# A pre-norm attention and gMLP block on one core: gated values kept in the gate's rows, other memory for the late operands, and program order on four engines to the end

## The chip, the cores and the metric

The kernel runs on 1 core of one Trainium2 chip. The metric is the device time of one execution in microseconds. The core's engines are PE (matrix products, with PEld for its weight loads), DVE, ACT and POOL (elementwise work), and SP, which here only issues transfers.

## The reference

One sequence of 2048 tokens of width 640 passes two blocks in fp32. The change touches the second block alone:

```python
def _A_ref(x, wqkv, wo): ...      # 32 heads of 20, causal window of 256, softmax, projection
def _B_ref(x, w_in, w_sp, b_sp, w_out):
    z = _gelu(jnp.einsum("bsd,df->bsf", x, w_in))           # 640 -> 1728
    z1 = z[..., :Fh]                                        # Fh = 864
    z2 = _layernorm(z[..., Fh:], axis=-1)
    g = jnp.einsum("ts,bsf->btf", w_sp, z2) + b_sp[None, :, None]   # 2048 x 2048 over tokens
    return jnp.einsum("bsf,fd->bsd", z1 * g, w_out)         # 864 -> 640
h = x + _A_ref(_layernorm(x), wqkv, wo)
h2 = h + _B_ref(_layernorm(h), w_in, w_sp, b_sp, w_out)
```

## The kernel before

Tokens lie in 16 tiles of 128. Every fp32 operand is split into a high part (`hi`, a copy on ACT) and a remainder (`lo`, a subtraction on DVE), and every product is three matmuls (high by high, high by low, low by high) into one PSUM bank. The big products use seven block products in place of eight; their operands are named B11, T1, T2, B22, T3, B21, T4.

The attention and the projection run first. Then the second block runs as a list `steps`: each step has a function that writes PE's matmuls and one, the post, that empties their bank. `at(n, f)` hangs other work (loads, copies, subtractions) on a step's number; `run(n)` writes first what hangs on n, then the matmuls of step n, then its post. The steps are:

- 0 to 63: `z_pair`, eight tile pairs, 8 steps each: the first halves z1 of z, written to `z1_d` in memory.
- 64 to 79: `z2_pair`, four pairs (0 to 3), 4 steps each. A step is 15 matmuls of 432 columns into one of four banks of tag "a". Its post is a gelu on ACT into a row buffer (`row`). The statistics of a row (`stat`, on DVE and POOL), its normalisation on ACT (`norm`) and the copies, remainders and subtractions for the seven pieces (`right_blocks`, into `zc`) hang on the steps behind. The operands of the next tile (`prep`: a copy into `aw` from `fx`, and the remainder) hang on steps before.
- 80 to 135: `first_gate`, eight pairs of row tiles of w_sp, 7 steps of 12 matmuls: the gate's products over the first half of the tokens, written to `g_d`. The copies, sums and remainders of w_sp (`preps`) go into `aw`, raw tiles into `fx`. They hang on steps up to 9 before the pair.
- 136 to 151: `z2_pair` again, pairs 12 to 15, over the second half of the tokens.
- 152 to 207: `second_gate`: the products over the second half, added on DVE to the rows read back from `g_d`; then `gated` adds the bias and multiplies with z1, which is loaded into the two buffers `z1` (printed as z); the result is stored to `y_d`. The preparation of w_out hangs on 31 of these steps.
- 208 to 263: `out_pair`, eight pairs, 7 steps: y is turned by transposes on PE, split, multiplied with w_out, and added to h.

Which order the engines get is set in two ways. Inside `manual_schedule`, PE, DVE, ACT and SP take the instructions in the order in which the code writes them. Behind `ms.close()` a list scheduler reorders them by its own estimates. Before the change that happens at step 62, so that all from the first z2 pair on is in the scheduler's order. An engine takes its instructions in the final order, one by one, each when its semaphores allow.

The block below prints the functions that the change touches and their callers.

Of the kernel before, what the change touches and what calls it, by code (L numbers as in the profile page):

```python
# [15 lines left out]
P = 128  # L16
# [18 lines left out]
def block_kernel(ctx, tc, x, xt, wqk, wv, wo, w_in, wsp, bsp, w_out, out):  # L35
# [89 lines left out]
    def view(flat, lo, *shape):  # L125
        n = 1
        for d in shape:
            n *= d
        names = "abcd"[:len(shape)]
        return flat[:, lo:lo + n].rearrange(f"p ({' '.join(names)}) -> p {' '.join(names)}",  # L130
                                            **dict(zip(names, shape)))
# [675 lines left out]
    def minus(out, a, b, eng=None):  # L807
        plus(out, a, b, OP.subtract, eng)

    def copy(out, a):  # L810
        nc.scalar.activation(out, a, AF.Copy)  # L811
# [86 lines left out]
    def open_d():  # L898
        early_stack.close()
        base_stack.close()  # L900
        zp = pool(zc_stack, "zc")
        z = [zp.tile([P, 2, HF], F32R, name=f"ze{n}") for n in range(12)] + zl
        zc.extend([z[7 * k:7 * k + 7] for k in range(4)])
        wp = pool(win_stack, "win2")
        win2.append(wp.tile([P, 2, KD, FH], F32R, name="win2"))

    def open_e1():
        win_stack.close()
# [111 lines left out]
    def z2_pair(q, i, j, k):  # L1020

        n0 = len(steps)
        f0 = 2048 if q == 12 else 0
        r = [view(fx, f0 + (2 * k + t) % 3 * D, D) for t in range(2)]
        a = [view(aw, 3328 + (2 * k + t) % 3 * 2 * D, 2, KD, P) for t in range(2)]
        z = [row(), row()]

        def prep(t, first):
            r3 = r[t].rearrange("p (k t) -> p k t", k=KD)
            if first:  # L1030
                copy(a[t][:, 0], r3)
            else:
                minus(a[t][:, 1], r3, a[t][:, 0].bitcast(F32))

        def prod(t, h, b):
            b.append(bank("a", f"zb{q}_{t}_{h}"))
            for kk in range(KD):
                for x, y in ((0, 0), (0, 1), (1, 0)):
                    nc.tensor.matmul(b[0][:, :HF], a[t][:, x, kk], win2[0][:, y, kk, h * HF:(h + 1) * HF],  # L1039
                                     start=kk + x + y == 0, stop=kk == KD - 1 and x == 1)  # L1040

        def gelu(t, h, b):
            with tc.high_priority() if q == 15 else ExitStack():
                nc.scalar.activation(z[t][:, h * HF:(h + 1) * HF], b.pop()[:, :HF], AF.Gelu_apprx_tanh)

        for t, tile_t in ((0, i), (1, j)):
            m = n0 + 2 * t
            soon = k == 0 and q > 8
            at(m - (8 if soon else 12 if k == 0 else 6), lambda t=t, tile_t=tile_t: nc.sync.dma_start(r[t], hn_d[tile_t]))
            at(m - (2 - t if soon else 3), lambda t=t: prep(t, True))  # L1050
            at(m - (1 if soon else 2), lambda t=t: prep(t, False))
        for t in range(2):
            for h in range(2):
                steps.append((lambda t=t, h=h, b=(b := []): prod(t, h, b), lambda t=t, h=h, b=b: gelu(t, h, b)))
        blocks = [x[:, h * HF:(h + 1) * HF] for x in z for h in range(2)]
        stats = [None, None]

        def stat(t, h):
            if h == 0:
                stats[t] = stat_tiles(f"z{q}_{t}")  # L1060
            st, mv = stats[t]
            nc.vector.bn_stats(out=st[:, h, :], in_=blocks[2 * t + h])
            if h:
                stats_of(mv, st)

        def norm(t):
            scaled(z[t], z[t], stats[t][1])

        f = right_blocks(lambda: zc[k], *blocks)
        def soon(n, *fs):  # L1070
            def run_all():
                with tc.high_priority() if q == 15 else ExitStack():
                    for x in fs:
                        x()

            at(n, run_all)

        soon(n0 + 1, lambda: stat(0, 0))
        soon(n0 + 2, lambda: stat(0, 1))
        soon(n0 + 3, lambda: stat(1, 0), lambda: norm(0), *f[:3])  # L1080
        soon(n0 + 4, lambda: stat(1, 1), lambda: norm(1), f[3])
        soon(n0 + 5, *f[4:])
# [4 lines left out]
    def gate_pair(p, c, post, extra):  # L1087

        n0 = len(steps)
        if p == 0:  # L1090
            e_start.append(n0)
        f0 = (p + 1) % 2 * 2048
        a11, a12, a21, a22 = (view(fx, f0 + o, 4, P) for o in (0, 512, 1024, 1536))
        s1 = view(tmp1, 0, 4, P)
# [19 lines left out]
        def s4():  # L1114
# [5 lines left out]
                 (-3, lambda: (s2(), lo(T1, s1), hi(T2, a11))), (-2, lambda: (lo(T2, a11), hi(T3, a21))),  # L1120
                 (-1, lambda: (lo(T3, a21), hi(B21, a12))), (0, lambda: (s4(), hi(T4, a22))),
                 (1, lambda: (lo(B22, a12), lo(T4, a22)))]
        if p == 0:
            preps = [(-9, lambda: hi(B11, a11)), (-8, lambda: (lo(B11, a11), s13())), (-7, lambda: (s2(), hi(T1, s1))),
                     (-6, lambda: (lo(T1, s1), hi(T2, a11))), (-5, lambda: lo(T2, a11)), (-4, lambda: hi(B21, a12)),
                     (-3, lambda: lo(B21, a12)), (-2, lambda: minus(a12, a12, a11)),
                     (0, lambda: (hi(B22, a12), hi(T3, a21))), (1, lambda: lo(B22, a12)),
                     (2, lambda: (lo(T3, a21), hi(T4, a22))), (3, lambda: lo(T4, a22))]
        if p == 1:
# [1 line left out]
                     (-2, lambda: (s2(), lo(T1, s1), hi(T2, a11))), (-1, lambda: (lo(T2, a11), hi(T3, a21))),  # L1131
                     (0, lambda: (lo(T3, a21), hi(B21, a12), s4(), hi(T4, a22))),
                     (1, lambda: (lo(B22, a12), lo(T4, a22)))]
        at(n0 - 11 if p != 1 else n0 - 10, load)
        for m, f in preps:
            at(n0 + m, f)

        def prod(m, half, start, stop):
            if m in (B11, T1):
# [215 lines left out]
    def second_gate(p):  # L1355
# [10 lines left out]
        def gated(n):  # L1366
            t, c = (p + 8, j) if n > 20 else (p, i)
            z = e1["z1"][c % 2][:, HF * (n % 10 - 1):HF * (n % 10)]
            nc.vector.scalar_tensor_tensor(out=z, in0=g[n], scalar=bcol[:, t:t + 1], in1=z, op0=OP.add, op1=OP.mult)

        def load_z(n):
            nc.sync.dma_start(e1["z1"][n % 2], z1_d[tile_of(n)])

        at(n0 - (5 if p else 1), lambda: nc.sync.dma_start(gi, g_d[p]))
        for c in (1, 0):
            at(n0 - (4 if p else 0), lambda c=slice(c * HF, (c + 1) * HF): nc.sync.dma_start(gj[:, c], g_d[p + 8][:, c]))
        at(n0 + (1 if p else 0), lambda: load_z(i))
        at(n0 + (2 if p else 0), lambda: load_z(j))
        at(n0 + (4 if p else 5), lambda: gated(12))
        at(n0 + (5 if p > 1 else 6), lambda: gated(22))  # L1380
        at(n0 + 6, lambda: gated(11))
        at(n0 + 7, lambda: gated(21))
        for t in range(2):
            at(n0 + 6 + t, lambda t=t: nc.sync.dma_start(y_d[p + 8 * t], e1["z1"][t]))
        gate_pair(p, 1, [add(11), add(22), add(12), add(12), add(22), add(11), add(21)], lambda m: None)
        if p == 0:
            for k in range(4):
# [91 lines left out]
    for n in range(len(steps)):  # L1479
        run(n)  # L1480
        if n == 0:
            turn_h(NT - 2)
        if n == 1:
            scale_h(NT - 1)
        if n == 5:
            turn_h(NT - 1)
        if n == 62:
            ms.close()
        if n == 6:
            open_d()  # L1490
            w2p = win2_prep(view(fx, 4 * D + 256, FH))
        if n > 10:
            next(w2p, None)
# [30 lines left out]
```

## Time and profile before

| | |
|---|---|
| median of 3 runs | 1121.25 us (1114.17 to 1122.6) |
| profiled execution | 1122.61 us, span 1120.9 us |
| mean granted clock of PE | 0.998 |
| busy PE / PEld / DVE / ACT / POOL | 1079.9 / 972.4 / 801.1 / 585.1 / 317.3 us |

Busy shares are of the span. A row with two numbers at its start gives start and duration in us; "x3" means three instructions merged; what stands in brackets is how long the engine was idle before, and which engine, tile and line released it. Matmuls are pipelined: one of 432 columns lasts 0.36 us in a row, but the next starts 0.2 us behind it.

### The profile page before, as it was taken

What the parts mean: (1) busy time and instruction counts of PE and PEld (TensorE: products, weight loads), DVE (VectorE), ACT (ScalarE), POOL (GpSimd) and SP (SyncE); (2) the same over time, 40 slices, a digit from 0 to 9 for tenths busy, and PEclk for the clock granted to TensorE, in tenths of its full rate; (3) what the DMA queues carried; (4) which work ended last, traced back from release to release, by engine and by line L of the source; (5) the groups of instructions that cost most, each with busy time, mean ns of one, the idle gap of its engine ahead of it and who ended that gap; (6) DMA issues with size and microseconds to landing.
All of it is one profiled execution on the core that took longest, in us unless ns stands there. A gap on an engine that the chain in (4) does not pass through costs nothing.

```text
span 1120.9 us, 28796 instructions
## 1 busy us (share of the span) xinstructions
PE 1079.9 (96%) x11083; PEld 972.4 (87%) x11083; DVE 801.1 (71%) x2185; ACT 585.1 (52%) x1202; POOL 317.3 (28%) x447
## 2 busy tenths in 40 slices
PE   8999999999998999998999999999999899999998
PEld 8998887667887787798899999999999798898998
DVE  6643444789998998697777678655458988787684
ACT  4444443259998899644566567433347532233231
POOL 4324446776676677632200011000001000000000
PEclk9999999999999999999999999999999999999999
DMA  7833667545665555789545422233241477656542
GB/s 244 297 113 119 173 185 266 172 162 180 185 191 179 179 172 168 189 256 315 208 167 196 157 88 76 86 123 111 99 156 57 161 217 262 205 189 238 176 139 94
DMA packets 92282, 194.74 MB, mean 174 GB/s; under 512 B 11952, under 2 KB 46272, under 8 KB 88256
## 3 DMA queue, kind: packets, MB, share of 16 engines
q1 hardware_dynamic: 92144, 192.90, 53.3%
q8 instruction: 87, 1.43, 0.5%
q14 instruction: 51, 0.42, 0.1%
HBM read 127.90 MB, written 64.95 MB: 172 GB/s over the span
## 4 chain that ended last, share of the span: by engine, by line
PE 35%; DMA 10%; DVE 9%; ACT 2%; issue 2%; SPq 1%; POOL 1%; DVEq 0%; ACTq 0%; POOLq 0%
PE g L1147 14%; PE zb L1039 4%; PE out_x L1311 4%; DMA fx<-wsp_in 3%; PE zx L987 2%; PE out_v L1311 2%; PE zv L987 2%; DVE aw L805 2%; DVE row L805 1%; PE zy L987 1%; DMA y_d<-z 1%; PE zw L987 1%; DMA fx<-y_d 1%; PE yt L1266 1%; PE wo_ps L102 1%
## 5 line engine op out<-in xcount | busy, mean ns | idle before, releaser
L398 ACT ACTIVATE pt<-bank 128x384 f32<-128x384 f32 (+1 forms) x452 | 179.6, 484 | 20.6 <-PE bank L395 14.1
L811 ACT ACTIVATE aw<-fx 128x512 fp32r<-128x512 f32 (+2 forms) x160 | 93.0, 595 | 150.1 <-PE g L1147 60.5
L1147 PE MATMUL g<-zl,aw 128*128 128x432 f32 x768 | 168.4, 357 | 0.1
L352 DVE CUSTOM_DVE_ANT_0 junk<-bank,strip 128x288 bf16<-128x288 f32 x392 | 157.3, 453 | 13.2 <-PE bank L342 10.0
L1147 PEld LDWEIGHTS g<-zl,aw 128*128 128x128 f32 x768 | 144.0, 188 | 6.5 <-DVE zl L805 0.4
L1147 PE MATMUL g<-ze,aw 128*128 128x432 f32 x576 | 133.3, 361 | 9.0 <-DVE row L805 8.6
L423 PE MATMUL pv<-pt,v_sb 128*32 128x192 f32 (+3 forms) x1984 | 134.6, 322 | 4.1 <-POOL pt L402 2.6
L805 DVE TENSOR_TENSOR aw<-fx,aw 128x512 fp32r<-128x512 f32 (+2 forms) x160 | 102.5, 646 | 38.3 <-ACT aw L811 37.3
L1147 PEld LDWEIGHTS g<-ze,aw 128*128 128x128 f32 x576 | 106.6, 188 | 18.8 <-DVE row L805 8.9
L402 POOL TENSOR_SCALAR_AFFINE_SELECT pt<-pt 128x512 f32<-128x512 f32 x128 | 83.6, 654 | 57.0 <-ACT pt L398 51.9
L342 PE MATMUL bank<-slot 120*32 120x288 bf16 (+5 forms) x1280 | 94.5, 274 | 3.7 <-issue 2.0
L395 PE MATMUL bank<-slot 123*32 123x288 bf16 (+6 forms) x1296 | 96.4, 273 | 0.7 <-ACT pt L398 0.7
L1039 PE MATMUL zb<-win,aw 128*128 128x432 f32 x480 | 95.3, 359 | 0.0
L88 POOL TENSOR_TENSOR mvz<-mvz,half 128x1 f32<-128x1 f32 x16 | 10.1, 632 | 299.9 <-DVE mvz L87 297.9
L1039 PEld LDWEIGHTS zb<-win,aw 128*128 128x128 f32 x480 | 89.9, 187 | 5.0 <-ACT row L811 0.3
L395 PEld LDWEIGHTS <-slot 123*32 123x32 bf16 x1728 | 62.2, 96 | 13.1 <-issue 4.1
L423 PEld LDWEIGHTS pv<-pt,v_sb 128*32 128x32 f32 x1984 | 63.9, 110 | 10.3 <-POOL pt L402 6.5
L805 DVE TENSOR_TENSOR row<-g,row 128x432 f32<-128x432 f32 x80 | 47.5, 602 | 34.0 <-PE g L1147 28.5
L405 POOL TENSOR_SCALAR_AFFINE_SELECT pt<-pt 128x512 f32<-128x512 f32 x112 | 71.0, 634 | 0.0
L342 PEld LDWEIGHTS <-slot 120*32 120x32 bf16 x1440 | 51.5, 95 | 14.2 <-issue 7.6
L352 DVE CUSTOM_DVE_ANT_0 junk<-bank,mask 128x384 bf16<-128x384 f32 (+2 forms) x120 | 51.0, 447 | 16.7 <-PE bank L346 15.6
L599 POOL TENSOR_TENSOR sg<-rest,sg 128x512 bf16<-128x512 f32 x40 | 46.7, 1168 | 56.9 <-ACT sg L598 46.3
(250 smaller groups left out, 2429.7 us busy)
## 6 DMA issues: line engine op xcount, KB each, us to landing
slot<-qk_d SPq DMA_DIRECT2D x144, 160.0 KB
fx<-wsp_in SPq DMA_DIRECT2D x32, 512.0 KB
qk_d<-sg SPq DMA_DIRECT2D x40, 384.0 KB
fx<-hn_d SPq DMA_DIRECT2D x32, 320.0 KB
o_d<-ot SPq DMA_DIRECT2D x64, 128.0 KB
xb<-qk_d SPq DMA_DIRECT2D x48, 160.0 KB
z_d<-row SPq DMA_DIRECT2D x16, 432.0 KB
g_d<-row SPq DMA_DIRECT2D x16, 432.0 KB
```

The lines of the kernel that those rows point to most:

```text
L342: nc.tensor.matmul(ps[32 * j:32 * j + 32, o:o + w], one(st, 120, 0, hh, q0, 32), k, start=True, stop=True, tile_position=(0, 32 * j))
L352: nc.vector.tensor_tensor_reduce(out=junk[:, :n], in0=ps[:, :n], in1=keep, scale=1.0, scalar=NEG, op0=OP.add, op1=OP.max, accum_out=m_cols ...
L395: nc.tensor.matmul(ps[32 * i:32 * i + 32, b + o:b + o + w], one(st, 123, 1, hh, k0, 32), q, start=True, stop=True, tile_position=(0, 32 * i))
L398: nc.scalar.activation(pt[:, hh, :n], ps[:, :n], AF.Exp, scale=SCALE)
L402: nc.gpsimd.affine_select(out=pt[:, :, :P], in_=pt[:, :, :P], pattern=[[0, 4], [1, P]], base=0, channel_multiplier=-1, compare_op=OP.is_ge ...
L405: nc.gpsimd.affine_select(out=pt[:, :, 256:], in_=pt[:, :, 256:], pattern=[[0, 4], [-1, P]], base=-1, channel_multiplier=1, compare_op=OP. ...
L423: nc.tensor.matmul(ps[32 * hh:32 * hh + 32, a - 512 * c:b - 512 * c], v_sb[:, kb, v0:v0 + 32], pt[:, hh, a - kb * P:b - kb * P], start=fir ...
L805: (eng or nc.vector).tensor_tensor(out=out, in0=a, in1=b, op=op)
L811: nc.scalar.activation(out, a, AF.Copy)
L987: nc.tensor.matmul(ps, a[x], b[:, y], start=start and m + x + y == 0, stop=stop and m == n - 1 and x == 1, skip_group_check=True)
L1039: nc.tensor.matmul(b[0][:, :HF], a[t][:, x, kk], win2[0][:, y, kk, h * HF:(h + 1) * HF], start=kk + x + y == 0, stop=kk == KD - 1 and x == 1)
L1147: nc.tensor.matmul(ps, w[m][:, x, k], zc[k][m][:, y], start=start and k + x + y == 0, stop=stop and k == 3 and x == 1, skip_group_check=True)
```

## The change

Four things are edited.

1. `gated` writes its result over the gate's row instead of over z1, and the rows are stored to `y_d`. Some loads hang on other steps.
2. The second four z2 pairs take their operands from new tiles, `z2_a` and `z2_r`, which lie in the space that `win2` is given up to later; the first four still use `aw` and `fx`.
3. The preparation of the second gate's first pair hangs 16 steps earlier, ahead of these z2 pairs (`early`, `e0`).
4. `ms.close()` at step 62 is gone: PE, DVE, ACT and SP take the written order to the end.

```diff
         win2.append(wp.tile([P, 2, KD, FH], F32R, name="win2"))
+        win2.append((wp.tile([P, 6 * D], F32R, name="z2_a"), wp.tile([P, 3 * D], F32, name="z2_r")))
...
     def z2_pair(q, i, j, k):
-        f0 = 2048 if q == 12 else 0
-        r = [view(fx, f0 + (2 * k + t) % 3 * D, D) for t in range(2)]
-        a = [view(aw, 3328 + (2 * k + t) % 3 * 2 * D, 2, KD, P) for t in range(2)]
+        late = q > 11
...
+        def raw(t):
+            return view(win2[1][1] if late else fx, (2 * k + t) % 3 * D, D)
+        def parts(t):
+            o = (2 * k + t) % 3 * 2 * D
+            return view(win2[1][0], o, 2, KD, P) if late else view(aw, 3328 + o, 2, KD, P)
...
     def gate_pair(p, c, post, extra):
+        early = p == 0 and c == 1
+        e0 = n0 - 16 if early else n0
...
-        if p == 0:
+        if p == 0 and c == 0:
             preps = [(-9, lambda: hi(B11, a11)), ...
...
-        at(n0 - 11 if p != 1 else n0 - 10, load)
+        at(e0 - 11 if p != 1 else n0 - 10, load)
         for m, f in preps:
-            at(n0 + m, f)
+            at(e0 + m, f)
...
     def second_gate(p):
         def gated(n):
-            nc.vector.scalar_tensor_tensor(out=z, in0=g[n], scalar=bcol[:, t:t + 1], in1=z, op0=OP.add, op1=OP.mult)
+            nc.vector.scalar_tensor_tensor(out=g[n], in0=g[n], scalar=bcol[:, t:t + 1], in1=z, op0=OP.add, op1=OP.mult)
...
-        at(n0 - (5 if p else 1), lambda: nc.sync.dma_start(gi, g_d[p]))
+        at(n0 - (3 if p else 1), lambda: nc.sync.dma_start(gi, g_d[p]))
         for c in (1, 0):
-            at(n0 - (4 if p else 0), lambda c=slice(c * HF, (c + 1) * HF): nc.sync.dma_start(gj[:, c], g_d[p + 8][:, c]))
+            at(n0 - (2 if p else 0), lambda c=slice(c * HF, (c + 1) * HF): nc.sync.dma_start(gj[:, c], g_d[p + 8][:, c]))
         at(n0 + (1 if p else 0), lambda: load_z(i))
-        at(n0 + (2 if p else 0), lambda: load_z(j))
+        at(n0 + (1 if p else 0), lambda: load_z(j))
...
-        for t in range(2):
-            at(n0 + 6 + t, lambda t=t: nc.sync.dma_start(y_d[p + 8 * t], e1["z1"][t]))
+        for t, r in enumerate((gi, gj)):
+            at(n0 + 7 + t, lambda t=t, r=r: nc.sync.dma_start(y_d[p + 8 * t], r))
...
-        if n == 62:
-            ms.close()
```

The first place where the order differs is ACT in the first z2 pairs. Names: zb is the bank of a z2 step (its two digits are tile and half), row 10086 and 10087 are the first pair's rows, 10088 the next pair's; ze 11047 to 11053 are the first pair's pieces B11, T1, T2, B22, T3, B21, T4; mvz holds a row's statistics; aw<-fx of 640 is the operand copy for a later tile. Before:

```order
L1044 ACTIVATE row_10086<-zb_0_1_11730 128x432
L811 ACTIVATE aw<-fx 128x640
L1044 ACTIVATE row_10087<-zb_1_1_11781 128x432
L93 ACTIVATE row_10086<-row_10086,mvz_0_11727 128x864
L811 ACTIVATE ze_11047<-row_10086 128x432
L1044 ACTIVATE row_10088<-zb_0_0_11811 128x432
L93 ACTIVATE row_10087<-row_10087,mvz_1_11772 128x864
L811 ACTIVATE ze_11048<-row_10086 128x432
L811 ACTIVATE ze_11052<-row_10087 128x432
L811 ACTIVATE ze_11050<-row_10087 128x432
```

After:

```order
L811 ACTIVATE ze_11048<-row_10086 128x432
L811 ACTIVATE aw<-fx 128x640
L1051 ACTIVATE row_10087<-zb_1_1_11782 128x432
L93 ACTIVATE row_10087<-row_10087,mvz_1_11773 128x864
L811 ACTIVATE ze_11052<-row_10087 128x432
L811 ACTIVATE ze_11049<-row_10086 128x432
L811 ACTIVATE ze_11050<-row_10087 128x432
L1051 ACTIVATE row_10088<-zb_0_0_11812 128x432
L811 ACTIVATE ze_11051<-row_10086 128x432
L811 ACTIVATE ze_11053<-row_10087 128x432
L811 ACTIVATE aw<-fx 128x640
L1051 ACTIVATE row_10088<-zb_0_1_11843 128x432
```

Before, every gelu (row<-zb) stands ahead of most pieces of the pair before it. After, the gelu of the first pair's fourth step (zb_1_1) stands behind the copy of T1 (11048) and an operand copy, the next pair's first (row 10088<-zb_0_0) behind the second normalisation and the copies of B21, T2 and B22, and its second behind those of T3 and T4.

The second place is DVE in the output. yt are the banks with turned y, out_x, out_y and out_v the banks of products, which are added to h in row or z; rows with 384 or 96x128 prepare the next pair's operands. One stretch of such a pair before:

```order
L805 TENSOR_TENSOR row_10088<-yt_1_1_14946,wo_raw_13539 128x384
L805 TENSOR_TENSOR row_10088<-row_10088,yt_0_0_14926 128x384
L805 TENSOR_TENSOR wo_raw_13539<-yt_0_0_14926,wo_raw_13539 128x384
L142 TENSOR_TENSOR zl_10080<-row_10088,zl_10080 128x384
L805 TENSOR_TENSOR row_10089<-out_v,row_10089 128x320
L142 TENSOR_TENSOR zl_10075<-yt_1_1_14946,zl_10075 96x128
L142 TENSOR_TENSOR zl_10081<-row_10088,zl_10081 128x384
L142 TENSOR_TENSOR zl_10083<-wo_raw_13539,zl_10083 128x384
L805 TENSOR_TENSOR z_0_13537<-out_x,z_0_13537 128x320
L805 TENSOR_TENSOR row_10088<-yt_0_1_14927,row_10088 128x384
L142 TENSOR_TENSOR zl_10085<-yt_1_1_14946,zl_10085 128x384
L805 TENSOR_TENSOR row_10089<-out_x,row_10089 128x320
```

After, for another pair:

```order
L805 TENSOR_TENSOR z_1_13545<-out_v,z_1_13545 128x320
L805 TENSOR_TENSOR row_10087<-yt_1_1_14814,tmp_10090 128x384
L805 TENSOR_TENSOR row_10087<-row_10087,yt_0_0_14794 128x384
L142 TENSOR_TENSOR aw<-row_10087,aw 128x384 x2
L805 TENSOR_TENSOR z_1_13545<-out_x,z_1_13545 128x320
L805 TENSOR_TENSOR tmp_10090<-yt_0_0_14794,tmp_10090 128x384
L142 TENSOR_TENSOR aw<-tmp_10090,aw 128x384
L805 TENSOR_TENSOR z_0_13544<-out_v,z_0_13544 128x320
L805 TENSOR_TENSOR z_1_13545<-out_y,z_1_13545 128x320
L805 TENSOR_TENSOR row_10087<-yt_0_1_14795,row_10087 128x384
L142 TENSOR_TENSOR aw<-row_10087,aw 128x384
L142 TENSOR_TENSOR aw<-yt_1_1_14814,aw 96x128
```

Before, the three subtractions and sums stand together, and the remainders (L142), each of which needs a copy by ACT, come later, with additions of products between them. After, each remainder stands directly behind the subtraction whose result ACT must first copy, and the additions for PE stand between these groups in the order of the steps.

The third is SP in the second gate: y_d<- are the stores of gated values, <-z_d the loads of z1, <-g_d the rows of the first gate. Before:

```order
L1384 DMA y_d<-z_0_13537 128x864
L1374 DMA row_10086<-g_d 128x864
L1099 DMA fx<-wsp_in 128x1024
L1376 DMA row_10087<-g_d 128x432
L1372 DMA z_0_13537<-z_d 128x864
```

After:

```order
L1393 DMA y_d<-row_10086 128x864
L1393 DMA y_d<-row_10087 128x864
L1381 DMA z_0_13544<-z_d 128x864
L1381 DMA z_1_13545<-z_d 128x864
L1108 DMA fx<-wsp_in 128x1024 x2
L1383 DMA row_10086<-g_d 128x864
L1385 DMA row_10087<-g_d 128x432 x2
```

Before, a buffer z is stored and then loaded again with other transfers between. After, both rows of a pair are stored, then both z loads follow, and then the weights and the rows of later pairs.

More of the change, by code (lines that the diff above doesn't have):

```diff
@@ L1022, in z2_pair @@
         n0 = len(steps)
-        f0 = 2048 if q == 12 else 0
-        r = [view(fx, f0 + (2 * k + t) % 3 * D, D) for t in range(2)]
-        a = [view(aw, 3328 + (2 * k + t) % 3 * 2 * D, 2, KD, P) for t in range(2)]
+        late = q > 11
         z = [row(), row()]
+        def raw(t):
[3 more added lines that the diff above has]
+            return view(win2[1][0], o, 2, KD, P) if late else view(aw, 3328 + o, 2, KD, P)
         def prep(t, first):
-            r3 = r[t].rearrange("p (k t) -> p k t", k=KD)
+            r3, a = raw(t).rearrange("p (k t) -> p k t", k=KD), parts(t)
             if first:
-                copy(a[t][:, 0], r3)
+                copy(a[:, 0], r3)
             else:
-                minus(a[t][:, 1], r3, a[t][:, 0].bitcast(F32))
+                minus(a[:, 1], r3, a[:, 0].bitcast(F32))
         def prod(t, h, b):
             b.append(bank("a", f"zb{q}_{t}_{h}"))
+            a = parts(t)
             for kk in range(KD):
                 for x, y in ((0, 0), (0, 1), (1, 0)):
-                    nc.tensor.matmul(b[0][:, :HF], a[t][:, x, kk], win2[0][:, y, kk, h * HF:(h + 1) * HF],
+                    nc.tensor.matmul(b[0][:, :HF], a[:, x, kk], win2[0][:, y, kk, h * HF:(h + 1) * HF],
                                      start=kk + x + y == 0, stop=kk == KD - 1 and x == 1)
@@ L1048, in z2_pair @@
             soon = k == 0 and q > 8
-            at(m - (8 if soon else 12 if k == 0 else 6), lambda t=t, tile_t=tile_t: nc.sync.dma_start(r[t], hn_d[tile_t]))
+            at(m - (8 if soon else 12 if k == 0 else 6), lambda t=t, tile_t=tile_t: nc.sync.dma_start(raw(t), hn_d[tile_t]))
             at(m - (2 - t if soon else 3), lambda t=t: prep(t, True))
```

## The prediction

> **What bounds the kernel now.** I read the stages of the part behind 642 us first, because the change touches only that part: the busy time of each engine in five stretches (second-half values z2, first gate, z2 again, second gate, output). Columns: stretch; its length; busy time and count of PE, PEld, DVE, ACT and POOL; clock; DMA share; GB/s.
>
> ```profile
> 642.00:689.40 47.40, 47.40 (x242) 44.79 (x241) 38.78 (x79) 32.96 (x56) 7.38 (x14) 1.00 0.27 87
> 689.40:820.60 131.20, 131.06 (x668) 124.80 (x667) 73.12 (x120) 51.58 (x95) 0.81 (x2) 1.00 0.31 104
> 820.60:868.90 48.30, 48.30 (x246) 45.90 (x245) 36.45 (x76) 30.55 (x53) 6.60 (x13) 1.00 0.29 94
> 868.90:1022.00 153.10, 142.33 (x727) 131.75 (x727) 125.41 (x233) 50.53 (x96) 1.83 (x4) 1.00 0.64 209
> 1022.00:1117.50 95.50, 94.03 (x660) 93.18 (x658) 67.59 (x153) 28.39 (x69) 0.00 (x0) 1.00 0.46 155
> ```
>
> PE is busy nearly without a break in the first three and in the last. In the second gate (868.90 to 1022.00) it is not. The first gate does its 672 products of 432 columns (668 fall into the stretch, with 4 of z2) in 131.2 us, 0.195 us each. The second gate has the same 672 and, within the stretch, 21 transposes and 33 output products, 7.0 us at the rates quoted under the output: 138.2 us of work in 153.1, so **14.9 us are lost there**. The waits of PE and those of SP, the queue that issues the transfers, say how (who waited for whom: total us, times, longest):
>
> ```profile
> PE g L1147 <- DVE row L805: 8.6, 7, 2.8
> ```
>
> ```profile
> SPq L1372 <- DMA y_d<-z: 34.7, 13, 5.2
> ```
>
> PE waits for DVE to empty its PSUM banks. SP waits 34.7 us until a store of gated values has left buffer z before it reloads z. The chain of work shows that loop once (start, length):
>
> ```profile
> 904.08 6.64 DMA y_d<-z
> ...
> 910.79 3.83 DMA z<-z_d
> ...
> 934.51 1.20 DVE aw L805 x2
> ```
>
> So today's order loses 15 us in one place. Everywhere else behind 642 us the schedule hides what DVE and ACT do, and the question is whether the written order hides it too.
>
> **The change part by part.** *Gated values into the gate's rows* ends the loop: z is free as soon as DVE has read it. *z2's second-half operands in other memory* frees aw and fx, so that the first pair of the second gate is prepared 16 steps earlier, in the last pair of the first gate, where DVE is busy 73.12 of 131.20 us. The memory itself costs nothing. It moves 11 DVE operations, 6.6 us at 0.60 (934.51: two in 1.20), and 7 ACT copies out of z2. In the second gate DVE then has per pair 11 of these, 7 additions at 0.52, 4 gated products at about 0.6, and for five pairs 2.5 us of w_out: 15.1 us beside 16.4 us of PE. It fits, with little room, so I take back 13.4 of the 14.9 us and leave 1.5; the ends are 14.9 (none left) and 0, where the written order brings new waits as long as the old ones. In SP's queue the two stores of a pair now stand ahead of the two loads of z, and the loads wait only for DVE's last gated product; behind them queue the weights of the pair after next and the next gate rows. From the first row of a pair's second step to the fifth, where z is needed, are 7 us, against the 3.83 us that a load took at 910.79, which is the cover of these transfers; if a load takes 3 us longer, DVE and then PE wait that long.
>
> *Program order* acts on z2 most. One z2 step is 15 products:
>
> ```profile
> 641.87 47.67 PE L1039 MATMUL zb<-win,aw 128*128 128x432 f32 x240
> ```
>
> 16 steps in 47.5 us: 2.97 us a step, 11.9 us a pair. Each step fills one of 4 PSUM banks, which a gelu on ACT empties. Until now ACT ran each gelu as soon as PE was done (656.99 below, released by PE). In the changed order the gelu of step 4 stands behind the copy of T1, and the gelus of the next pair's steps 1 and 2 behind the copies of B22 and T4, and each of these copies waits for DVE, which waits for ACT. Both engines take their rows one by one, so a pair becomes one chain. Its links, from the rows of the first pair today:
>
> ```profile
> 654.49 0.51 ACT L1044 ACTIVATE row<-zb 128x432 f32<-128x432 f32 x1
> 654.90 1.10 ACT L93 ACTIVATE row<-row,mvz 128x864 f32<-128x864 f32 x1
> 656.03 0.57 ACT L811 ACTIVATE ze<-row 128x432 fp32r<-128x432 f32 x1
> 656.99 0.53 ACT L1044 ACTIVATE row<-zb 128x432 f32<-128x432 f32 x1 [0.39 <-PE zb L1039]
> 657.99 1.11 ACT L93 ACTIVATE row<-row,mvz 128x864 f32<-128x864 f32 x1 [0.48 <-POOL mvz L89]
> 659.01 1.91 ACT L811 ACTIVATE ze<-row 128x432 fp32r<-128x432 f32 x4
> 660.83 0.72 ACT L811 ACTIVATE aw<-fx 128x640 fp32r<-128x640 f32 x1
> 661.46 0.51 ACT L1044 ACTIVATE row<-zb 128x432 f32<-128x432 f32 x1
> ```
>
> ```profile
> 655.36 0.60 DVE L1062 BATCH_NORM_STATS2 stz<-row 128x6 f32<-128x432 f32 x1
> ...
> 656.63 0.63 DVE L805 TENSOR_TENSOR ze<-row,ze 128x432 fp32r<-128x432 f32 x1 [0.17 <-ACT ze L811]
> 657.30 0.61 DVE L805 TENSOR_TENSOR row<-row 128x432 f32<-128x432 f32 x1
> ...
> 659.13 0.61 DVE L805 TENSOR_TENSOR row<-row,row 128x432 f32<-128x432 f32 x1 [0.70 <-ACT row L93]
> 659.66 1.12 DVE L805 TENSOR_TENSOR ze<-row,ze 128x432 fp32r<-128x432 f32 x2
> 660.70 0.60 DVE L805 TENSOR_TENSOR row<-row,row 128x432 f32<-128x432 f32 x1
> ...
> 662.78 0.82 DVE L805 TENSOR_TENSOR aw<-fx,aw 128x640 fp32r<-128x640 f32 x1
> 663.51 0.60 DVE L1062 BATCH_NORM_STATS2 stz<-row 128x6 f32<-128x432 f32 x1
> ```
>
> From the statistics of a second half (655.36) over two tiny DVE and two POOL operations to the normalisation (657.99): 2.63 us. Normalisation to copy (654.90 to 656.03) 1.13; copy to remainder (656.03 to 656.63) 0.60; remainder to subtraction (656.63 to 657.30) 0.67; subtraction to the next copy 0.60 (1049.77 on DVE to 1050.37 on ACT, below). That is 5.63 us to the copy of T1. Then 0.46 for it (659.01, four in 1.82), 0.63 for the operand copy (660.83 to 661.46), and 0.60 from gelu to statistics: 1.69. Statistics again 2.63 and normalisation to subtraction (657.99 to 659.13) 1.14: 3.77. Two subtractions and the operand remainder (0.52, 0.52, 0.73), two remainders (1.04), a third and the subtraction up to the copy of T4 (0.52, 0.60): 3.93. Copy of T4, operand copy, gelu and statistics: 1.69. Sum **16.7 us a pair, against 11.9 of PE**.
>
> The end, counted from PE's start of z2: the first second-half statistics stand at 6.8 (two steps, 0.28 drain, 0.60). In the first z2, three pairs follow at 16.7, 19.6 (the gate's preparation adds three DVE operations and two copies to the chain) and 17.3, then 12.1 to the remainder of B21, and 3.2 until T4 is copied and the gate's first bank is emptied behind it: 75.7. PE would be there at 54.6 (47.5, 33 gate products, three more): **21.0 us late**. In the second z2: 6.8, three times 16.7, 12.1, and 3.3 until DVE has added the gate's first bank: 72.3, **17.7 us late**. Together 38.7. The lower end is 0: DVE's own work, 38.78 us of 47.40 in the first stretch, would fit if no engine waited for another. The upper is 46, with 1 us more a pair.
>
> The Trainium skill (VectorE: DVE Perf Modes, The DRAIN you can't avoid) says that a DVE operation starts only when the pipe of the one before is empty. The trace speaks against it here: two remainders start at 659.66 and the next operation at 660.70, 0.52 apart, though each lasts 0.60. By the page's rule the chain would be some 0.5 us longer a pair, and the sum about 3 us higher (an estimate).
>
> In the output a pair has 75 products and 14 transposes:
>
> ```profile
> 1053.98 0.93 PE L1266 MATMUL yt<-ident,fx 128*128 128x128 f32 x7
> 1054.66 1.56 PE L1311 MATMUL out_v<-wo,aw 128*128 128x320 f32 x9
> 1056.06 0.61 PE L1317 MATMUL out_v<-wo,aw 96*128 96x320 f32 x3
> 1056.51 1.49 PE L1311 MATMUL out_x<-wo,zl 128*128 128x320 f32 x9
> ```
>
> 0.15 and 0.097 us each: 12.6 us a pair, 93.8 us left at 1022.00, so today's stretch loses 1.7. In the written order DVE makes sums, remainders and additions of PE's results in one line, and the next pair's second product needs the bank that the pair's last addition empties.
>
> ```profile
> 1049.77 0.56 DVE L805 TENSOR_TENSOR row<-yt,wo_raw 128x384 f32<-128x384 f32 x1
> 1050.37 0.56 DVE L805 TENSOR_TENSOR row<-row,yt 128x384 f32<-128x384 f32 x1
> ...
> 1051.30 0.55 DVE L142 TENSOR_TENSOR zl<-row,zl 128x384 fp32r<-128x384 f32 x1
> 1051.77 0.48 DVE L805 TENSOR_TENSOR row<-out_v,row 128x320 f32<-128x320 f32 x1
> 1052.17 0.28 DVE L142 TENSOR_TENSOR zl<-yt,zl 96x128 fp32r<-96x128 f32 x1
> ```
>
> ```profile
> 1050.37 0.53 ACT L141 ACTIVATE zl<-row 128x384 fp32r<-128x384 f32 x1 [5.76 <-DVE row L805]
> ```
>
> From the end of a pair's fourth product: 0.28 drain, addition 0.40, plus 0.60, three subtractions with copy and remainder (each 0.60, 0.57, 0.47), one more remainder 0.47, addition 0.40, two additions 0.80, small remainder 0.20, last addition 0.49: 8.6 us. PE reaches the bank after 45 products, 6.7 us. So **1.9 us a pair, seven times, 13.2; less the 1.7: 11.5 more** (ends 0, if DVE's turns fall into PE's, and 17, with late loads of h).
>
> Sum: 38.7 - 13.4 + 11.5 = **36.8 us longer**. The profiled execution has a span of 1120.9 and took 1122.61, so 1159.4; the median of the runs shown lies 1.4 lower: **1158**.
>
> **The rivals.** *Faster.* If ACT's late gelus stay within the four banks in z2, and the output's additions within theirs, only the gate's 14.9 us go: 1107. It decides at the z2 chain: with 3 repeats in 54.6 us the chain must be below 11 us a pair for no wait, and near 13 us for the gate's gain to pay for it if the output costs nothing. For it speaks that DVE and ACT have idle time in every stretch; against it that 6.4 of the 16.7 us are two passes through statistics, POOL and normalisation which no order inside the engine shortens. *The clock.* After the long waits PE may run slower:
>
> ```profile
> 540.00:550.00 10.00, 8.16 (x48) 7.94 (x47) 9.55 (x21) 5.74 (x10) 2.30 (x4) 0.83 0.37 146
> ```
>
> ```profile
> 542.74 0.53 PE L102 MATMUL wo_ps<-xb 128*128 128x320 f32 x2 [1.84 <-DVE xh L1425]
> ```
>
> The granted clock (third number from the end) was 0.83 over 10 us in which PE had waited 1.84 us: 1.7 us lost. The Trainium skill (TensorE: Matmul & The Clock Gate, What's actually happening) puts the drop to half clock behind an idle window of about 3.4 us; here a shorter wait was enough. My z2 has waits of about 5 us. Most slow products would lie in time that PE waits anyway; two ends of z2 at 1.7 us make 1161, all six long waits 1168. *Less than the whole chain.* If POOL's hop is quicker and one z2 half is hidden by two thirds: 1122 + 37 - 22, 1137. *Nothing.* If the second gate stays at 15.1 DVE against 16.4 PE with new waits for its row loads, and z2 costs little, gain and loss cancel within 1%, about what a measurement of this kernel can tell.
>
> **How the numbers follow.** Forecast 0.58 (1142 to 1170); clock or further waits beyond it 0.10 (1161 to 1180); less than the whole chain 0.14 (1133 to 1142); no change 0.08; faster 0.10 (1107). Slower by over 1% is the sum of the first three, 0.82. The range 1130 to 1175 leaves out faster, most of no change and the far end of the clock.
>
> **What would show it.** In the new profile both z2 stretches become longer than 60 us from the first z2 product to the first gate's fourth; PE's longest waits there are for DVE (operands, the pieces of z2) and ACT (gelu's banks). The DVE wait of PE in the second gate falls below 3 us and SP's wait for the gated stores goes. The output takes over 105 us. I am wrong if ACT's gelus run within 3 us of PE in z2, and wrong in the second term if the second gate still takes 150 us.

## The result, and the profile after

The changed kernel takes **1153.18 us** (median; 1147.67 to 1158.13) against 1119.76 us (1114.17 to 1122.6) of the kernel before, run beside it: a ratio of **1.0307, 95% interval 1.0278 to 1.0336**. The profiled execution took 1150.68 us with a span of 1149.0, so 28.1 us more than the profiled execution of before. The forecast was 1158.

The first view is the busy time by stretch, as in the prediction, but cut where the terms of the sum were counted: from z2's first product to T2, the first gate product that needs a copied-out bank; the first gate from there to z2's second stage; that stage to its T2; the second gate; the output.

```profile
638.11:712.28 74.17, 60.77 (x278) 55.37 (x276) 47.39 (x93) 40.31 (x69) 8.17 (x16) 0.91 0.20 67
712.28:839.37 127.09, 126.39 (x636) 120.77 (x637) 70.09 (x113) 46.91 (x85) 0.00 (x0) 0.99 0.34 117
839.37:909.92 70.55, 57.94 (x278) 53.26 (x276) 44.44 (x89) 37.41 (x63) 7.89 (x16) 0.93 0.27 89
909.92:1039.43 129.51, 128.56 (x651) 122.44 (x651) 114.38 (x204) 39.83 (x77) 0.00 (x0) 0.98 0.62 218
1039.43:1145.70 106.27, 102.42 (x699) 98.82 (x697) 73.90 (x162) 30.75 (x73) 0.00 (x0) 1.00 0.43 152
```

PE's work in a stretch up to T2 is 54.6 us. It took 74.2 and 70.6, and the granted clock (third number from the end) is 0.91 and 0.93 there. The timeline of PE shows where PE stood (the bracket: idle time ahead of the row, and what ended it):

```profile
638.11 18.31 PE L1046 MATMUL zb<-win,aw 128*128 128x432 f32 x92
657.51 12.13 PE L1046 MATMUL zb<-win,aw 128*128 128x432 f32 x60 [1.09 <-DVE aw L805]
674.32 14.31 PE L1046 MATMUL zb<-win,aw 128*128 128x432 f32 x60 [4.68 <-DVE aw L805]
693.21 8.49 PE L1046 MATMUL zb<-win,aw 128*128 128x432 f32 x28 [4.58 <-DVE aw L805]
...
712.28 2.10 PE L1156 MATMUL g<-ze,aw 128*128 128x432 f32 x6 [2.43 <-ACT row L811]
...
909.92 2.53 PE L1156 MATMUL g<-ze,aw 128*128 128x432 f32 x6 [2.65 <-DVE row L805]
```

Three waits in each z2 stage are for an operand whose remainder stands in DVE's queue behind the pieces of the pair before; then PE waits at T2 for a bank that ACT (first z2) or DVE (second) empties, behind the last pieces. The list of waits has the sums:

```profile
PE zb L1046 <- DVE aw L805: 10.4, 3, 4.7
...
PE zb L1046 <- DVE z_a L805: 7.6, 3, 4.4
```

What DVE and ACT did meanwhile is one chain. This is the chain of work that ended last, in order of time (start, length, engine, what, line), from one second-half statistics to that of the next pair, with a few links left out:

```profile
652.24 0.62 DVE stz L1069
...
653.50 0.56 POOL mvz L88
...
654.45 1.12 ACT row L93
...
657.46 1.55 DVE ze L805 x3
...
659.57 0.57 ACT ze L811
...
660.77 1.06 DVE stz L1069 x2
...
662.47 1.02 POOL mvz L88
...
663.88 1.12 ACT row L93
665.02 0.57 ACT ze L811
...
666.90 0.57 ACT ze L811
...
668.62 0.42 ACT row L1051
669.06 0.62 DVE stz L1069
```

From 652.24 to 669.06 are **16.82 us**, in which each row is released by the one ahead of it, on its own engine or on another: statistics on DVE, the power on POOL, normalisation on ACT (2.21 us later), remainders and a subtraction on DVE, a copy on ACT, then the next pair's statistics of its first tile, POOL again, normalisation again, a copy (665.02) with its remainder and a subtraction, the copy of the result (666.90) and two operand copies, and only then the gelu (668.62) that the next statistics need. PE's products are in none of these links.

In the second gate SP's wait for the stores of gated values (34.7 us before) is gone; SP's queue waits for DVE's gated products instead, off PE's path:

```profile
SPq L1393 <- DVE row L1378: 55.2, 12, 10.4
```

The account, stage by stage, with work counted at the prediction's rates (0.195 us a product, 12.6 us a pair of the output):

| stretch | lost before | lost after | change | forecast |
|---|---|---|---|---|
| first z2 to T2 | 0 | 19.6 | +19.6 | +21.0 |
| first gate behind T2 | 0 | 2.9 | +2.9 | 0 |
| second z2 to T2 | 0 | 16.0 | +16.0 | +17.7 |
| second gate | 14.9 | 3.9 | -11.0 | -13.4 |
| output | 1.7 | 6.8 | +5.1 | +11.5 |
| ahead of z2 (start at 641.87 and 638.11) | | | -3.8 | 0 |

The sum is 28.8 beside the 28.1 of the spans. The last line isn't the change's: the second profiled execution of the unchanged kernel (below) also starts z2 at 638.2. Against that one the span is 33.5 us longer, as the medians are (33.4).

### The profile page after: what moved, and what is told of

It is laid out like the page before. It is cut to its first block, busy times and chain, and to the rows that moved or that the text cites. A ratio compares the mean times of both kernels' runs of the same rounds, so it can differ in the third digit from the quotient of the medians.

```text
span 1149.0 us, 28801 instructions
## 1 busy us (share of the span) xinstructions
PE 1090.1 (95%) x11083; PEld 980.1 (85%) x11083; DVE 809.4 (70%) x2185; ACT 586.3 (51%) x1202; POOL 317.2 (28%) x447
## 4 chain that ended last, share of the span: by engine, by line
PE 37%; DVE 11%; ACT 5%; DMA 4%; issue 2%; POOL 1%; SPq 0%; POOLq 0%; DVEq 0%; ACTq 0%
PE g L1156 21%; DVE row L805 3%; PE out_x L1320 3%; PE zx L988 2%; PE zv L988 2%; DVE zl L805 2%; ACT row L93 2%; PE zb L1046 2%; PE zy L988 1%; PE wo_ps L102 1%; PE zw L988 1%; DMA m<-o_d 1%; PE yt L1275 1%; PE out_v L1320 1%; DVE stz L1069 1%
## 5 line engine op out<-in xcount | busy, mean ns | idle before, releaser
L1156 PE MATMUL g<-zl,aw 128*128 128x432 f32 x768 | 171.0, 361 | 3.0 <-ACT zl L811 1.8
L811 ACT ACTIVATE aw<-fx 128x512 fp32r<-128x512 f32 (+2 forms) x152 | 85.7, 585 | 98.2 <-DVE fx L805 75.9
L1156 PEld LDWEIGHTS g<-ze,aw 128*128 128x128 f32 x576 | 108.9, 190 | 13.5 <-DVE row L805 5.3
L805 DVE TENSOR_TENSOR aw<-fx,aw 128x512 fp32r<-128x512 f32 (+2 forms) x152 | 94.4, 637 | 26.2 <-ACT aw L811 26.2
L1046 PE MATMUL zb<-win,aw 128*128 128x432 f32 x240 | 53.2, 385 | 10.4 <-DVE aw L805 10.4
L1046 PEld LDWEIGHTS zb<-win,aw 128*128 128x128 f32 x240 | 48.9, 205 | 14.5 <-DVE aw L805 11.8
```

The costliest lines, as they stand in the source:

```text
L805: (eng or nc.vector).tensor_tensor(out=out, in0=a, in1=b, op=op)
L1046: nc.tensor.matmul(b[0][:, :HF], a[:, x, kk], win2[0][:, y, kk, h * HF:(h + 1) * HF], start=kk + x + y == 0, stop=kk == KD - 1 and x == 1)
L1156: nc.tensor.matmul(ps, w[m][:, x, k], zc[k][m][:, y], start=start and k + x + y == 0, stop=stop and k == 3 and x == 1, skip_group_check=True)
```

## The experiments

The theory: in program order z2 is one chain over ACT, DVE and POOL, 16.7 us a pair; that, and not PE's banks, DVE's work or program order as such, makes the kernel slower, and the edits to the second gate win back some 11 us. The runs bear out the first half; of the second only a part. Ratios are to the kernel before, run beside each on the same chip, at about 1118 us.

**Program order alone, and the edits alone.** The first is the kernel of before without the line that ends program order; the second is the kernel of after with it.

```diff
-        if n == 62:
-            ms.close()
```

> The kernel of before with program order to the end, without the other edits. My theory: the order costs what the trace of after shows (z2 35.5 us in its two stretches, 2.6 in the first gate, 5.0 in the output), and the loop of store and reload in the second gate is a matter of memory, not of order, so its 14.9 us stay: 1120 + 43 = 1163, some 11 us above after, with SP still waiting for stores of gated values. Rival: the order itself ends the wait in the second gate, and the other edits do nothing: 1153, as after.

> The kernel of after with the scheduler's order put back from step 62 on. My theory: no chain in z2, and the second gate loses 3 to 4 us instead of 14.9: 1120 - 11 = 1109, between 1104 and 1113. Rival: without the written order the scheduler puts new waits into the second gate (its DVE work is 114 of 130 us in after), and nothing is won: 1116 to 1122.

Program order alone: 1157.12 us (1155.44 to 1159.29), ratio 1.036 (1.033 to 1.0389). The edits alone: 1118.51 (1111.59 to 1120.22), ratio 0.999 (0.9969 to 1.0011). So order costs about 40 us; the edits win some 6 under it (1.036 - 1.0307 = 0.0053; the two intervals just overlap, and the two profiled spans differ by 4.7) and, in the timed runs, nothing that can be told under the scheduler. My expectation for the first, 11 us above after, was off, and its trace says why:

```profile
914.46 2.53 PE L1147 MATMUL g<-ze,aw 128*128 128x432 f32 x6 [3.85 <-DVE row L805]
```

T2 of the second z2 comes at 914.46, 75.6 us after that stage's start at 838.87 (PE's timeline); after has 70.55. **5.0 of the 5.9 us lie here**, in z2: without its own memory for late operands the gate's preparation stays in the chain, and this stage takes about as long as the first (74.2). From T2 to the output are 130.3 us, after has 129.5. So in the second gate program order alone wins the lost time back (4.7 us stay lost there, 3.9 in after), although SP still waits for stores of gated values, for 12.7 us in place of 34.7:

```profile
SPq L1372 <- DMA y_d<-z: 12.7, 7, 3.1
```

Why the order alone shortens that wait, no run here shows. With the edits alone the loop came back in another place: the rows of the next pair's gate values are now loaded into memory that the stores of gated values still read.

```profile
SPq L1385 <- DMA y_d<-row: 14.8, 6, 5.0
SPq L1383 <- DMA y_d<-row: 10.2, 6, 2.4
```

25.0 us in place of 34.7. PE, however, waits less. These are its waits for DVE behind the z2 stages, over the second profiles that follow, first of before and then of the edits alone:

```profile
PE g L1147 <- DVE row L805: 5.2, 4, 2.8
```

```profile
PE g L1156 <- DVE row L805: 2.9, 2, 1.9
```

In the first profiles they are 8.6 and 2.0 us. The edits' profiled execution (1111.59) was shorter than most of its timed runs, so it and before were compared over further executions:

> A second profile of the kernel of after with the scheduler's order from step 62 on. Its first profiled execution had a span of 1109.9 though its median was 1118.5. If the edits save the second gate's loss in every execution, this one has again a second gate some 10 us shorter than before's; if that profile was the lucky end of the scatter, the gate takes about as long as in before, with waits for the gate's rows.

> A second profile of the kernel of before, unchanged. It shows how far one execution stands for the others: if the 14.9 us lost in the second gate are there again, they belong to the kernel; if they are 5 or less, they were an accident of the execution that the prediction was worked out from, and part of the gain that was booked there was never to be had.

> The kernel of after with the scheduler's order from step 62 on, timed once more, in more rounds and on another chip. Its two profiled executions (1111.6 and 1113.0) showed z2 to the end in 465.9 and 468.1 us against 475.7 and 474.0 in the two of before, but its timed runs had a median of 1118.5, the same as before's. If the edits are worth what the profiles show, the ratio is 0.994 (some 7 us); if they are worth nothing, it is 0.999 again.

The second profiled execution of before took 1117.23 us. Its span is 1115.5, z2 to the end takes 474.0 us (475.7 in the first), and SP's wait is there again (32.1 us in the same view): the loss belongs to the kernel. The edits' second profile took 1113.03, and the timing 1115.24 (1108.95 to 1117.96), ratio 0.998 (0.9959 to 1.0002). In all three of its profiles z2 to the end takes 466 to 468 us, 6 to 10 less than in the two of before, and the timed medians show 2 of them at most (the intervals end at 0.9959, 4.6 us). Where the rest goes in unprofiled runs can't be seen; it **stays open**.

**The scheduler in z2 only.**

```diff
+        if n in (62, 134):
+            ms.close()
+        if n in (83, 155):
+            ms.enter_context(tc.manual_schedule(engines={
+                mybir.EngineType.PE, mybir.EngineType.DVE, mybir.EngineType.Activation, mybir.EngineType.SP}))
```

> The kernel of after, but the scheduler orders the two z2 stages (steps 63 to 83 and 135 to 155), and the written order is taken up again behind each. My theory: the whole loss of z2 sits in the order of these steps, so both stretches fall from 74.2 and 70.6 us to about 55, and what the slow clock and the late gate rows cost behind them (2.6 and 2 us) goes too: 1153 - 39 = 1114. Rival: the operands of the gate's first pair, which are prepared in the same steps, hold PE up in any order: 1140 or more.

1115.5 us (1113.2 to 1119.85), ratio 0.9985 (0.9966 to 1.0003): 36 us less than after, 39 expected. T2 of the first z2 comes at 691.49 in PE's timeline, 54.9 us after z2's start at 636.63, where PE's work alone takes 54.6. The normalisations (L93) of the first two pairs in ACT's timeline show what the order does:

```profile
649.67 1.10 ACT L93 ACTIVATE row<-row,mvz 128x864 f32<-128x864 f32 x1
...
652.75 1.11 ACT L93 ACTIVATE row<-row,mvz 128x864 f32<-128x864 f32 x1 [0.47 <-POOL mvz L89]
...
662.21 1.11 ACT L93 ACTIVATE row<-row,mvz 128x864 f32<-128x864 f32 x1 [0.60 <-POOL mvz L89]
...
664.24 1.10 ACT L93 ACTIVATE row<-row,mvz 128x864 f32<-128x864 f32 x1
```

The two normalisations of a pair follow each other within 2.0 to 3.1 us, with waits of half a microsecond for POOL; in after (654.45 and 663.88 in the chain) a pair's two are 7 us apart and these two, of neighbouring pairs, 9.4, and ACT waits 2.2 to 2.3 us ahead of each.

**Is it the chain or what PE waits for?** Two runs. One lengthens a link that no other row needs, POOL's tiny last operation; the other gives PE more banks and the operands that it was seen waiting for earlier.

```diff
                 stats_of(mv, st)
+                for _ in range(4):
+                    nc.gpsimd.tensor_scalar(out=mv[:, 2:3], in0=mv[:, 0:1], scalar1=mv[:, 3:4], scalar2=-1.0,
+                                            op0=OP.mult, op1=OP.mult)
```

> The kernel of after with POOL's last tiny operation of each half's statistics (0.26 us, 0.36 from one start to the next) done five times instead of once; the result is the same. POOL itself is idle there more than nine tenths of the time. My theory: a pair is one chain and both hops lie on it, so each of the 8 halves of a z2 stage adds 1.44 us: 11.5 us a stage, 23 in all, 1176 us, and a pair takes 19.7 us where it took 16.8. Rival: the loss is the work of DVE and ACT in program order, and the hop is hidden behind other rows: less than 8 us, under 1161.

1177.3 us (1172.33 to 1178.96), ratio 1.0524 (1.0491 to 1.0557), 24 us more than after. The second normalisations of the first two pairs, in ACT's timeline, and T2 in PE's:

```profile
658.87 1.11 ACT L93 ACTIVATE row<-row,mvz 128x864 f32<-128x864 f32 x1 [3.67 <-POOL mvz L1073]
...
678.55 1.11 ACT L93 ACTIVATE row<-row,mvz 128x864 f32<-128x864 f32 x1 [3.67 <-POOL mvz L1073]
```

```profile
725.29 2.53 PE L1159 MATMUL g<-ze,aw 128*128 128x432 f32 x6 [2.00 <-ACT row L811]
```

658.87 to 678.55 is 19.68 us a pair (19.7 expected, 16.82 in after), and T2 comes 85.5 us after z2's start at 639.81, 11.3 more than in after (11.5 expected). Four more operations of 0.27 us, which lengthen ACT's wait for POOL from 2.24 to 3.67 us, on an engine that is busy 8.2 of the stage's 74.2 us in after, are paid in full, eight times a stage.

```diff
-            b.append(bank("a", f"zb{q}_{t}_{h}"))
+            b.append(bank("ab"[t], f"zb{q}_{t}_{h}"))
-            at(m - (2 - t if soon else 3), lambda t=t: prep(t, True))
-            at(m - (1 if soon else 2), lambda t=t: prep(t, False))
+            at(m - (2 - t if soon else 4), lambda t=t: prep(t, True))
+            at(m - (1 if soon else 3), lambda t=t: prep(t, False))
```

> The kernel of after, with z2's products in eight PSUM banks instead of four, and each operand prepared one step earlier, which are the two things that PE waits for in z2 itself. My theory: the pieces of z2 come off the chain of ACT, DVE and POOL no earlier, so PE ends z2 sooner and waits as much longer in the gate's first steps; T2 still starts 72 to 75 us (first z2) and 69 to 72 us (second) after z2's start, and the time stays within 1148 to 1156. Rival: the loss is PE's waits for banks and operands, 18 us in after's trace: with them the time falls to 1135 or less.

1149.85 us (1147.35 to 1154.61), ratio 1.0293 (1.0254 to 1.0332). PE's timeline:

```profile
636.42 30.15 PE L1046 MATMUL zb<-win,aw 128*128 128x432 f32 x152
...
709.88 2.53 PE L1156 MATMUL g<-ze,aw 128*128 128x432 f32 x6 [2.00 <-ACT row L811]
```

PE does 152 products in one go where it did 92 and ends the first z2 8.4 us earlier, counted from its start. One wait for an operand is left (4.66 us), and then PE waits for pieces and a bank; T2 is at 73.5 us after z2's start (74.2 in after), and at 70.0 in the second stage. The waits moved, the end did not.

**Program order with the rows laid out otherwise.** Both kernels keep program order and only hang z2's rows on other steps (and prepare operands one step earlier, as above).

```diff
-        soon(n0 + 3, lambda: stat(1, 0), lambda: norm(0), *f[:3])
-        soon(n0 + 4, lambda: stat(1, 1), lambda: norm(1), f[3])
-        soon(n0 + 5, *f[4:])
+        soon(n0 + 3, lambda: stat(1, 0), lambda: norm(0), f[0])
+        soon(n0 + 4, f[1], lambda: stat(1, 1), lambda: norm(1))
+        soon(n0 + 5, *f[2:5])
+        soon(n0 + 7, *f[5:])
```

> The kernel of after, in program order throughout, with only z2's rows at other steps: operands prepared a step earlier, half of the second statistics' work and the subtractions one step later, the last two pieces two steps later, so that no engine's next row waits for a hop over POOL. My theory: it is the chain (16.8 us a pair in the trace of after) and not program order as such, so the loss goes as it does under the scheduler: T2 at 55 to 58 us after z2's start in place of 74.2 and 70.6, 1114 to 1120. Rival: in program order ACT and DVE, busy 47 and 40 of PE's 55 us there, cannot keep up however the rows are laid: half of the loss stays, 1132 or more.

1129.81 us (1128.81 to 1131.37), ratio 1.011 (1.0086 to 1.0134): 22 us less than after where I expected 33 to 39. PE did all of z2 without a wait, but T2 came 62.6 and 60.0 us after its start, because, as I read it, ACT still waited 1.3 to 3.3 us for POOL ahead of each normalisation but the first of a stage. The longest of these in ACT's timeline:

```profile
690.52 1.11 ACT L93 ACTIVATE row<-row,mvz 128x864 f32<-128x864 f32 x1 [3.33 <-POOL mvz L89]
```

The second try puts the rows of all pairs but the last further apart, in place of the same three lines:

```diff
+        tail = q in (11, 15)
+        for m, *fs in ([(3, lambda: stat(1, 0)), (4, lambda: norm(0), lambda: stat(1, 1), *f[:2], lambda: norm(1)),
+                        (5, *f[2:6]), (6, f[6])] if tail else
+                       [(4, lambda: norm(0), f[0]), (5, lambda: stat(1, 0), lambda: stat(1, 1), f[1], lambda: norm(1)),
+                        (6, *f[2:4]), (7, *f[4:6]), (8, f[6])]):
+            soon(n0 + m, *fs)
```

> The kernel of after in program order throughout, with z2's rows laid out once more: for all pairs but the last of each stage both normalisations come a step later than in the first attempt and the last pieces two; for the last pair the rows stay close together, because the gate waits for them. My theory: the 8.0 and 5.4 us that the first attempt still lost ahead of T2 are waits of ACT for POOL and of DVE for the normalisation that followed too closely, so T2 comes 57 to 60 us after z2's start and the time is 1118 to 1123. Rival: they are the last pair's own chain, or the work of the two engines, and no order of rows helps: 1128 to 1131, as the first attempt.

1120.31 us (1117.26 to 1124.64), ratio 1.003 (1.0011 to 1.0048). T2 of the first z2 in PE's timeline:

```profile
638.51 47.51 PE L1046 MATMUL zb<-win,aw 128*128 128x432 f32 x240
...
696.58 2.53 PE L1159 MATMUL g<-ze,aw 128*128 128x432 f32 x6 [2.42 <-ACT row L811]
```

58.1 us after the start at 638.51, and 57.4 in the second; ACT now waits for POOL ahead of none of the sixteen normalisations. Of the 35.6 us lost in the two stages 6.3 are left; the kernel with the scheduler in z2 is 5 us faster (0.0045). Program order as such costs no more than that here, and the places of its rows cost the other 29.

**The output, and the best of both.** The scheduler from step 200 on, first on the kernel of after as shown, then together with the edit that gave the scheduler z2.

```diff
+        if n == 200:
+            ms.close()
```

> The kernel of after with the scheduler's order from step 200 on, the last pair of the second gate, so that the output alone is taken out of program order. By the trace of after the output loses 6.7 us to its written order against 1.7 under the scheduler: 1153 - 5 = 1148. By the prediction's term it would be 11.5 less, 1142. Rival: the order of the output costs nothing, and PE's waits there only take the place of others: 1153.

> The kernel of after with the scheduler's order in both z2 stages and from step 200 on, and program order in the two gates: each stage in the order that lost less. If the terms add, 1115.5 - 5 = 1110.5 against 1118 before, a ratio of 0.993. Rival: what the output wins under the scheduler is lost where the last gate pair and the output now mix, as in before's trace: 1115 to 1118.

The first: 1144.13 us (1143.51 to 1145.53), ratio 1.0251 (1.0225 to 1.0276), so 0.0056 or 6.3 us less than after, nearer to the 5 read from the trace than to the 11.5 of the prediction. The second: **1108.73 us (1104.27 to 1112.18), ratio 0.9933 (0.9907 to 0.9959)**, faster than both kernels, as the terms add up to: each stage has the order that lost less in it.

## Why the prediction was right, point by point

**z2, +38.7.** Found 35.6, by the mechanism named. The pair's chain was summed to 16.7 us from before's rows and measured 16.82; with the gate's preparation 19.6 was forecast, and 671.27 to 690.15 (normalisations, after's timeline of ACT) is 18.9. The link from statistics to normalisation, 2.63 twice in the sum, took 2.21 (652.24 to 654.45) and 2.66 (to 663.88 from the second of the two statistics, which DVE's timeline has from 660.69, 1.13 long at 0.60 each); the other links together were 0.5 longer. PE's waits are the two kinds named. By the one sentence that the prediction took from the Trainium skill (VectorE: DVE Perf Modes, The DRAIN you can't avoid) the chain would be an estimated 17.2; the same section adds that a next operation which isn't held starts earlier, and the trace agrees with that: three remainders in 1.55 us (657.46) start 0.52 apart though each lasts 0.60. So the trace speaks against that sentence read alone and not, as the prediction has it, against the page.

**Second gate, -13.4.** The size was nearly right (11.0), in part by luck, because its cause was only half right. I booked it to the gated values in the gate's rows, which end the reload loop. Program order alone brings it too: 130.3 us against 129.5 with the edits. Under the scheduler the edits turn SP's wait for z into one for the rows; PE's waits for DVE fall there as well (8.6 and 5.2 us in the profiles of before, 2.0, 2.9 and 2.3 with the edits alone), but the timed runs don't show the gain. So either part can shorten PE's waits, and the two don't add. The step that failed is "so I take back 13.4 of the 14.9 us" as the edits' work; what the edits bring under program order, 5.9 us, lies in z2, where of the edits only the separate memory and the earlier preparation act, which I had counted in z2's second term (17.7 in place of 21.0).

**Output, +11.5.** Found 5.1 in the trace and 6.3 by the experiment. The step that failed is "the next pair's second product needs the bank that the pair's last addition empties". In after's timelines that product starts before the addition:

```profile
1067.54 1.48 PE L1320 MATMUL out_x<-wo,aw 128*128 128x320 f32 x9
...
1078.90 1.13 PE L1320 MATMUL out_x<-ze,aw 128*128 128x320 f32 x6 [0.23 <-DVE row L805]
...
1080.73 1.49 PE L1320 MATMUL out_x<-wo,zl 128*128 128x320 f32 x9
1082.06 1.49 PE L1320 MATMUL out_y<-wo,zl 128*128 128x320 f32 x9
```

```profile
1078.26 0.48 DVE L805 TENSOR_TENSOR row<-out_x,row 128x320 f32<-128x320 f32 x1
...
1082.95 0.48 DVE L805 TENSOR_TENSOR row<-out_x,row 128x320 f32<-128x320 f32 x1
```

PE starts out_y at 1082.06, DVE adds the last out_x at 1082.95. What PE does wait for is nearer: T4 accumulates into x, which DVE must have read after T3 (1078.26), 0.23 us a pair. A pair takes 13.19 us (1067.54 to 1080.73 in PE's timeline) where I had 14.5. All of PE's listed waits in this stretch come to 4.5 us; what makes up the rest of the 6.8 isn't shown.

**The clock**, a rival, came true in part, beside the mechanism of the forecast. The granted clock is 0.91 and 0.93 in the z2 stretches, and behind the waits products are slow: 28 took 8.49 us in z2 where the stage's first 92 took 18.31, and the six at 909.92 took 2.53. Behind the two T2, where PE is on the path, that makes 1.7 of the 2.9 us in the first gate (another 0.7 is a wait for a row of DVE) and 2.1 of the 3.9 in the second; within z2 the chain hides it, since PE still waits 2.43 us at T2 behind them.

**The total.** 1158 against 1153.2: the output was 6.4 too dear and z2 3.1, the second gate was 2.4 too good, the first gate's 2.9 were missing, and the median of before is 1.5 lower in the runs beside. The terms' errors partly cancelled. The rivals "less than the whole chain" and "faster" fell with the lengthened link: 11.3 of the 11.5 us added to POOL's hop came out at T2. The signs named ahead were there: z2 over 60 us, ACT's gelus more than 3 us behind PE (that of the sixth step starts at 660.66 in ACT's timeline, an estimated 5.0 us after the step's last product, by 0.195 us a product from 638.11), PE's wait for DVE behind the second T2 0.87 us, SP's wait for the gated stores gone, the output 106.3; this last says little, since without the scheduler all eight pairs fall into that stretch.

## What to carry to other kernels

When an order written by hand replaces a scheduler, follow one unit of work through all engines and add the links from row to row; if that chain is longer than the unit's time on the busiest engine, each unit costs the difference, however idle the engines are. More buffers and earlier operands for the engine that waits only moved such a wait here; moving rows of one unit behind rows of the next took most of it away. And when a change has several parts, undo each alone before saying which one brought a gain: here the gain booked to one part came with the other part alone as well.

## What the runs showed of the hardware

POOL's tiny power takes 0.55 us, and about 1.0 beside some DVE operations. POOL's and DVE's timelines of after:

```profile
863.88 1.04 POOL L88 TENSOR_TENSOR mvz<-mvz,half 128x1 f32<-128x1 f32 x1 [8.19 <-DVE mvz L87]
...
896.47 0.55 POOL L88 TENSOR_TENSOR mvz<-mvz,half 128x1 f32<-128x1 f32 x1 [8.03 <-DVE mvz L87]
```

```profile
863.68 0.83 DVE L805 TENSOR_TENSOR z_a<-z_r,z_a 128x640 fp32r<-128x640 f32 x1
...
896.24 0.60 DVE L1069 BATCH_NORM_STATS2 stz<-row 128x6 f32<-128x432 f32 x1
```

Beside a subtraction with two inputs (863.68) it takes 1.04 us; beside statistics with one input (896.24) 0.55, as when DVE is idle. On this chain that is up to 0.5 us a pair. The Trainium skill (SBUF — State Buffer, SBUF: two separate sides) says that VectorE, with two inputs in that memory, and GpSimd lock each other out of a shared pair of ports; the rows agree.

The clock doesn't follow the length of the waits alone. Two executions of the unchanged kernel, at the same place of the second gate (PE's timeline, the first profile of before and then the second):

```profile
889.34 1.44 PE L1147 MATMUL g<-ze,aw 128*128 128x432 f32 x6 [2.78 <-DVE row L805]
...
893.66 1.41 PE L1147 MATMUL g<-ze,aw 128*128 128x432 f32 x6 [1.70 <-DVE row L805]
```

```profile
886.62 1.45 PE L1147 MATMUL g<-ze,aw 128*128 128x432 f32 x6 [2.82 <-DVE row L805]
887.90 2.31 PE L1147 MATMUL g<-zl,aw 128*128 128x432 f32 x6
890.93 2.50 PE L1147 MATMUL g<-ze,aw 128*128 128x432 f32 x6 [0.71 <-DVE row L805]
```

After waits of 2.78 and 1.70 us six products took 1.44 and 1.41 us, and the six at 890.62 between them 1.33. In the second profile the six after a wait of 2.82 took 1.45, but the next six 2.31, ahead of the wait of 0.71, and those behind it 2.50. The Trainium skill (TensorE: Matmul & The Clock Gate, What's actually happening) says that the activity is judged in a window of about 3.4 us that runs freely, so that it depends on where in the window work falls; that two nearly equal places came out differently agrees with it, and it means that such a loss can't be forecast from the waits alone.
